# Output products regrouped by kind, and the first two periods of an attention stage rearranged

## The chip, the cores and the metric

The kernel runs on one core of one Trainium2 chip. The metric is device time in microseconds: the median of several executions. A profiled execution has a span (first to last instruction) and a time of its own, which is a little longer.

## The reference

The kernel computes a linear attention with exponential features and, behind it, a two-layer block. The two weight matrices of the block arrive as float64.

```python
# q, k, v: (8 batches, 8 heads, 576 positions, 64); w_phi: (64, 128)
def phi(x):
    proj = einsum('bhsd,df->bhsf', x, w_phi)
    proj = proj - max(abs(proj), axis=-1)
    return concatenate([exp(proj), exp(-proj)], axis=-1)
q_p, k_p = phi(q), phi(k)
kv = einsum('bhsf,bhsd->bhfd', k_p, v)
z = sum(k_p, axis=2)
num = einsum('bhsf,bhfd->bhsd', q_p, kv)
den = einsum('bhsf,bhf->bhs', q_p, z) + 1e-06
x = (num / den), laid out as (4608, 512)
h = x @ w_in            # (512, 2048)
out = (h - tanh(h)) @ w_out
```

## The kernel before

**Two stages.** The attention takes roughly the first third of the time, the two-layer block the rest. Only the attention is touched.

**Units.** A unit is one batch and two heads (index e); there are 32 (`NU`). Its input `qk` holds the transposed queries and keys of both heads, 64 partitions a head and 2 x 576 columns; `v` holds the values. A unit's work goes through three periods of one loop, `for i in range(NU + 2)`: in period i, unit i (`a`) is projected, unit i-1 (`c`) is turned, summed and exponentiated, and unit i-2 (`p`) gets its outputs. The loop runs under a manual schedule: every engine takes its instructions in the order in which the loop writes them, and SP, which issues all transfers, takes them in that order too.

**One period's steps, by engine.**

- `project(a, r)`, r = 0, 1, 2: on TensorE six float32 products, which the profile shows as twelve instructions, into the one PSUM tile `pp`; then on VectorE a maximum of absolute values (`m`) and a subtract (`t`). As there is one tile `pp`, block r+1 on TensorE waits for the subtract of block r.
- `k_exp` (ScalarE): exponents of the keys, into `kp`. Its second half, `k_exp(c, 2)`, is issued in the next period.
- `kv(c)` (TensorE): keys times values, twenty instructions, needs all of `kp`. `ksum(c)`: sums of the keys' features.
- `qt`, `qt_rest`, `q_exp` (TensorE and ScalarE): transposes of the queries and their exponents `qe`, for both signs s and both heads e.
- `kv_copy`, `kv_turn`: ScalarE copies the keys-times-values out of PSUM, TensorE transposes them, VectorE copies the result to `kv`.
- `out_heads(p)` (TensorE): for each sign s, the numerators (L265: two column halves c and two heads e, 64 output columns each, PSUM tiles 0 and 1) and then the denominators (L275: four strips of 32 columns of PSUM tile 2). Each is accumulated over s. A float32 product shows as two instructions, so a block of four is eight.
- `out_copy`, `den`, `den_recip`, `den_mul`: copies to SBUF, a transfer `dn`, a reciprocal, a transfer out (`rr`) and two back (`rb`), a product on GpSimd and the store of x to DRAM (`xs`). The second stage reloads x from there.
- `dec_load`, `dec_0`, `dec_1`, `dec_2`: in each period one block of a float64 weight is loaded (`raw`, two buffers) and turned into float32: one ScalarE operation, then three of VectorE (`dec_1`), then one more of VectorE (`dec_2`). All 32 blocks are done within the attention.

**The start.** `wph` (the two copies of w_phi) is loaded first, then `qk` of unit 0, its `v`, and two weight blocks. Eight products of a tile of zeros, `zt`, are pinned in front of everything on TensorE (L134, bfloat16, 256 columns, into the PSUM tile `pw`, which nobody reads).

Of the kernel before, what the change touches and what calls it, by code (L numbers as in the profile page):

```python
# [32 lines left out]
def tile_linear_attention_moe(  # L33
# [73 lines left out]
    def x_split(xt, c, order=lambda ins: ins):  # L107
        xh, xl, x = xt
        order(nc.scalar.copy(xh[:, c, :], x[c]))
        order(nc.vector.tensor_tensor(xl[:, c, :], x[c], f32(xh[:, c, :]), ALU.subtract))  # L110
# [5 lines left out]
    with ExitStack() as c1:  # L116
# [6 lines left out]
        ps_c = c1.enter_context(tc.tile_pool(name="ps_c", bufs=1, space=PSUM))  # L123
        ps_d = c1.enter_context(tc.tile_pool(name="ps_d", bufs=3, space=PSUM))

        wph = p1.tile([P, F], F32, name="wph")
        nc.sync.dma_start(wph[0:D, :], w_phi)
        nc.sync.dma_start(wph[D:P, :], w_phi)
        zt = p1.tile([P, 256], BF16, name="zt")
        nc.gpsimd.memset(zt, 0.0)  # L130

        pw = ps_d.tile([P, 512], F32, tag="po", name="warm")
        for _ in range(8):
            pin(nc.tensor.matmul(pw[:, 0:256], zt[:, 0:P], zt, start=True, stop=True))  # L134

        ones = p1.tile([P, 32], F32, name="ones")
        nc.vector.memset(ones, 1.0)
# [5 lines left out]
        def dec_load(n):  # L143
            u = Dec()
            u.nm = f"{'io'[n % 2]}{n // 2}"
            u.f, u.d = n // 2, (wi, wo)[n % 2]
            u.r = raw.tile([P, DM], U64, tag="raw", name=f"raw{u.nm}")
            if n % 2 == 0:
                nc.sync.dma_start(
                    u.r.rearrange("p (c f) -> p c f", f=P),  # L150
                    w_in[:, u.f * P : (u.f + 1) * P].rearrange("(c p) f -> p c f", p=P),
                )
            else:
                nc.sync.dma_start(u.r, w_out[u.f * P : (u.f + 1) * P, :])
            return u

        def dec_0(u):
            rr = u.r.bitcast(U32).rearrange("p (n t) -> p n t", t=2)
            u.lo, u.hi = rr[:, :, 0], rr[:, :, 1]
            u.a = raw.tile([P, DM], U32, tag="dec_a", name=f"dec_a{u.nm}", bufs=2)  # L160
            nc.scalar.activation(f32(u.a), f32(u.hi), AF.Abs, scale=65536.0)

        def dec_1(u):
            a = u.a
            nc.vector.tensor_scalar(f32(a), f32(a), CMIN, CMAX, ALU.max, ALU.min)
            nc.vector.tensor_scalar(a, a, 3, None, ALU.logical_shift_left)
            nc.vector.scalar_tensor_tensor(a, u.lo, 29, a, ALU.logical_shift_right, ALU.bitwise_or)

        def dec_2(u):
            w = wpool.tile([P, DM], F32, tag="w", name=f"w{u.nm}")  # L170
            nc.vector.scalar_tensor_tensor(
                w.bitcast(U32), u.hi, 0x80000000, u.a, ALU.bitwise_and, ALU.bitwise_or
            )
            u.d[u.f] = w
# [3 lines left out]

        def load(u):
            u.qk = p2.tile([P, PC], F32, tag="qk", name=f"qk{u.i}")  # L180
            nc.sync.dma_start(u.qk, qkT[u.i])

        def load_v(u):
            u.v = p2.tile([P, 5, 2, D], F32, tag="v", name=f"v{u.i}")
            nc.sync.dma_start(u.v.rearrange("p j e d -> p (j e d)"), v5[u.i])


        def project(u, r):
            pp = ps_pj.tile([P, 2, 512], F32, tag="pj", name=f"pp{u.i}_{r}")
            for a in range(3):  # L190
                j = 3 * r + a
                for e in range(2):
                    hs = slice(e * D, (e + 1) * D)
                    nc.tensor.matmul(  # L194
                        pp[:, e, a * F : (a + 1) * F], u.qk[hs, j * P : (j + 1) * P], wph[hs, :], start=True, stop=True
                    )
            x = pp[:, :, 0 : 3 * F].rearrange("p e (a f) -> p e a f", f=F)
            m = p2.tile([P, 2, 3], F32, tag="m", name=f"m{u.i}_{r}")
            nc.vector.tensor_reduce(m, x, AX.X, ALU.max, apply_absolute_value=True)  # L199
            t = p2.tile([P, 2, 3, F], F32, tag=f"t{r}", name=f"t{u.i}_{r}")  # L200
            nc.vector.tensor_tensor(t, x, m.unsqueeze(3).broadcast_to([P, 2, 3, F]), ALU.subtract)  # L201
            u.t[r] = t
# [28 lines left out]
        def kv(u):  # L231
            u.pc = ps_c.tile([P, 512], F32, tag="pc", name=f"pc{u.i}")
            for j in range(5):
                r = slice(SR, P) if j == 0 else slice(0, P)
                for e in range(2):
                    nc.tensor.matmul(  # L236
                        u.pc[e * D : (e + 1) * D, 0 : 2 * F], u.v[r, j, e, :], u.kp[r, e, j, :, :], start=(j == 0), stop=(j == 4)
                    )
# [21 lines left out]
        def out_heads(u):  # L260
            u.po = [ps_d.tile([P, 512], F32, tag="po", name=f"po{u.i}_{c}") for c in range(3)]
            for s in range(2):
                for c in range(2):
                    for e in range(2):
                        nc.tensor.matmul(  # L265
                            u.po[c][e * D : (e + 1) * D, 0:CH],
                            u.kv[:, s, e * D : (e + 1) * D],
                            u.qe[:, e, s, c * CH : (c + 1) * CH],
                            start=(s == 0),
                            stop=(s == 1),  # L270
                        )
                for e in range(2):
                    for c in range(2):
                        n, w = 2 * e + c, 2 * e + s
                        nc.tensor.matmul(  # L275
                            u.po[2][n * 32 : (n + 1) * 32, 0:CH],
                            u.kv[:, 2, w * 32 : (w + 1) * 32],
                            u.qe[:, e, s, c * CH : (c + 1) * CH],
                            start=(s == 0),
                            stop=(s == 1),  # L280
                        )
# [27 lines left out]
        def den_mul(u, pin=lambda ins: ins):  # L309
            x = u.rb  # L310
            pin(nc.gpsimd.tensor_tensor(x, u.d, x, ALU.mult))  # L311
            nc.sync.dma_start(xs[u.b // 2][u.hp, :, (u.b % 2) * S : (u.b % 2 + 1) * S], x)
# [7 lines left out]
        NU = len(units)  # L320
        assert NU == 2 * NF
        load(units[0])
        load_v(units[0])
        dec = [dec_load(0), dec_load(1)]
        def unit(i):
# [3 lines left out]
        with tc.manual_schedule():  # L329
            for i in range(NU + 2):  # L330
                a, c, p, p2_ = unit(i), unit(i - 1), unit(i - 2), unit(i - 3)
                if i + 1 < NU:
                    load(units[i + 1])
                    load_v(units[i + 1])
                if i == NU:
                    xt = {0: x_tiles(0)}
                    for j in range(NCT):
                        x_load(0, xt[0], j)
                if a:
                    a.kp = p2.tile([P, 2, 5, 2, F], F32, tag="kp", name=f"kp{i}")  # L340
                    project(a, 0)
                if c and i < NU:
                    k_exp(c, 2)
                if p:
                    out_heads(p)
                if c and i == NU:
                    k_exp(c, 2)
                if i < NU:
                    dec_0(dec[i])
                    dec_1(dec[i])  # L350
                if p:
                    out_copy(p)
                    den(p)
                if p2_:
                    den_mul(p2_)
                if a:
                    project(a, 1)
                if c:
                    kv(c)
                if a:  # L360
                    k_exp(a, 1)
                if i < NU:
                    dec_2(dec[i])
                if i + 2 < NU:
                    dec.append(dec_load(i + 2))
                if i == NU:
                    for j in range(NCT):
                        x_split(xt[0], j)
                if a:
                    project(a, 2)  # L370
                if c:
                    c.qe = p1.tile([P, 2, 2, S], F32, tag="qe", name=f"qe{i - 1}")
                    pt = qt(c, 0)
                    q_exp(c, 0, pt)
                    ksum(c)
                    ptr = qt_rest(c)
                    kv_copy(c)
                    q_exp_rest(c, ptr)
                    pt = qt(c, 1)
                    kv_turn(c)  # L380
                    q_exp(c, 1, pt)
                if p:
                    den_recip(p)
                if i == NU:
                    split_w(0)
            for f in range(1, AHEAD):
                split_w(f)
# [150 lines left out]
```

## Time and profile before

| | us |
|---|---|
| median of 3 executions (lowest, highest) | 1226.46 (1226.25, 1227.1) |
| profiled execution, its time | 1227.16 |
| profiled execution, its span | 1225.4 |
| TensorE busy (matmul) | 1192.7 |
| VectorE busy | 895.6 |
| ScalarE busy | 800.9 |
| GpSimd busy | 273.2 |

In the profile PE is TensorE's products, PEld its weight loads, DVE VectorE, ACT ScalarE, POOL GpSimd, SP the engine that issues transfers. Starts are microseconds from the span's start, and L265 is line 265 of the kernel. Products are pipelined, so that the durations of neighbours overlap and the step from start to start is the better price. The chain of waits follows the last instruction back, at each step to what released it.

### The profile page before, as it was taken

The numbers are of one execution on the slowest core, as the hardware profiler recorded it, in microseconds if no ns is written. First come the engines' busy times: TensorE is split into PE (matmuls) and PEld (weight loads), VectorE is DVE, ScalarE is ACT, GpSimd is POOL, SyncE is SP. The second block draws the span as 40 slices with busy tenths as digits, with TensorE's granted clock in tenths as the row PEclk, the third lists the DMA queues.
The fourth block names the chain that finished last, engine by engine and source line by source line (L and its number), as shares of the span: only waits on it lengthen the run. The fifth ranks groups of instructions, "written<-read, shape, count | busy, mean of one in ns | idle before, by whom it ended". The sixth has DMA issues, their size and how long they took to land.

```text
span 1225.4 us, 22381 instructions
## 1 busy us (share of the span) xinstructions
PE 1192.7 (97%) x8552; PEld 962.8 (79%) x8552; DVE 895.6 (73%) x1478; ACT 800.9 (65%) x1709; POOL 273.2 (22%) x253
## 2 busy tenths in 40 slices
PE   5999999999999799999999999999999999999998
PEld 4565665665655688999999999999999999999997
DVE  5778778877775898767777777677677777777765
ACT  2665665656655676767776776776676776776665
POOL 0011111110111653222222222222222222222222
PEclk9999999999999999999999999999999999999999
DMA  4465566655653100001010000000010100000000
GB/s 157 123 195 169 172 186 177 175 174 166 199 164 113 45 14 29 20 11 39 14 40 14 33 20 33 14 33 20 7 39 14 39 14 33 21 26 1 27 1 27
DMA packets 50892, 85.70 MB, mean 70 GB/s; under 512 B 13280, under 2 KB 27744, under 8 KB 50784
## 3 DMA queue, kind: packets, MB, share of 16 engines
q1 hardware_dynamic: 50784, 84.27, 22.4%
q8 instruction: 67, 1.10, 0.4%
q14 instruction: 41, 0.34, 0.1%
HBM read 65.08 MB, written 19.02 MB: 69 GB/s over the span
## 4 chain that ended last, share of the span: by engine, by line
PE 92%; DVE 4%; ACT 1%; DMA 1%; issue 1%; SPq 0%; DVEq 0%
PE ph L407 31%; PE po L441 10%; PE po L442 10%; PE po L444 10%; PE pp L194 7%; PE pc L236 6%; PE po L265 5%; PE pc L244 3%; PE po L275 3%; PE ptt L207 3%; DVE s L424 1%; PE ptk L255 1%; PE ptr L213 1%; DVE s L428 1%; DVE s L423 0%
## 5 line engine op out<-in xcount | busy, mean ns | idle before, releaser
L435 POOL TENSOR_TENSOR gl<-s,gh 128x384 fp32r<-128x384 f32 x192 | 197.2, 1027 | 592.9 <-ACT gh L434 582.2
L407 PE MATMUL ph<-xh,wli 128*128 128x384 f32 x768 | 259.7, 338 | 3.5 <-POOL wli L92 3.5
L407 PE MATMUL ph<-xh,whi 128*128 128x384 f32 x768 | 259.3, 338 | 0.9 <-DVE th L427 0.9
L407 PE MATMUL ph<-xl,whi 128*128 128x384 f32 x768 | 258.5, 337 | 0.0
L414 ACT ACTIVATE y<-ph 128x384 f32<-128x384 f32 x192 | 94.3, 491 | 231.9 <-PE ph L407 231.9
L441 PE MATMUL po<-who,gh 128*128 128x512 f32 x576 | 228.7, 397 | 7.9 <-ACT gh L434 7.8
L423 DVE SCALAR_TENSOR_TENSOR s<-s,y 128x384 f32<-128x384 f32 x192 | 111.0, 578 | 166.9 <-ACT s L416 166.8
L442 PE MATMUL po<-wlo,gh 128*128 128x512 f32 x576 | 227.5, 395 | 0.0
L444 PE MATMUL po<-who,gl 128*128 128x512 f32 x576 | 164.1, 393 | 0.0
L407 PEld LDWEIGHTS ph<-xh,whi 128*128 128x128 f32 x768 | 144.8, 188 | 10.1 <-issue 1.7
L428 DVE COPY_PREDICATED s<-mk,th 128x384 f32<-128x384 uint32 x192 | 136.5, 711 | 20.0 <-DVE th L427 0.5
L407 PEld LDWEIGHTS ph<-xl,whi 128*128 128x128 f32 x768 | 144.6, 188 | 8.2
L407 PEld LDWEIGHTS ph<-xh,wli 128*128 128x128 f32 x768 | 144.5, 188 | 4.3 <-POOL wli L92 4.2
L228 ACT ACTIVATE kp<-t 128x768 f32<-128x768 f32 (+1 forms) x128 | 87.2, 733 | 68.5 <-DVE t L201 68.5
L199 DVE TENSOR_REDUCE m<-pp 128x6 f32<-128x768 f32 x96 | 91.8, 956 | 54.0 <-PE pp L194 53.9
L441 PEld LDWEIGHTS po<-who,gh 128*128 128x128 f32 x576 | 108.2, 188 | 28.8 <-ACT gh L434 11.7
L422 ACT ACTIVATE mk<-y,bias_t 128x384 f32<-128x384 f32 x192 | 117.8, 613 | 19.0 <-DVE s L428 19.0
L424 DVE SCALAR_TENSOR_TENSOR s<-s,s 128x384 f32<-128x384 f32 x192 | 115.1, 599 | 18.9 <-ACT mk L422 0.9
L444 PEld LDWEIGHTS po<-who,gl 128*128 128x128 f32 x576 | 108.4, 188 | 25.3
L311 POOL TENSOR_TENSOR rb<-d,rb 128x576 f32<-128x576 f32 x32 | 47.2, 1474 | 347.8 <-DMA rb<-rr 344.1
L442 PEld LDWEIGHTS po<-wlo,gh 128*128 128x128 f32 x576 | 108.6, 189 | 16.5
L416 ACT ACTIVATE s<-y,bias_t 128x384 f32<-128x384 f32 x192 | 118.4, 617 | 0.0
(63 smaller groups left out, 1660.8 us busy)
## 6 DMA issues: line engine op xcount, KB each, us to landing
qk<-in_qkT SPq DMA_DIRECT2D x32, 576.0 KB, 4.8
v<-in_v SPq DMA_DIRECT2D x32, 320.0 KB, 8.0
rb<-rr SPq DMA_DIRECT2D x64, 144.0 KB, 2.9
xs<-rb SPq DMA_DIRECT2D x32, 288.0 KB, 2.1
x<-xs SPq DMA_DIRECT2D x48, 192.0 KB, 2.3
out<-o SPq DMA_DIRECT2D x36, 256.0 KB, 2.1
rawi<-in_moe_w_in SPq DMA_DIRECT2D x16, 512.0 KB, 4.4
rawo<-in_moe_w_out SPq DMA_DIRECT2D x16, 512.0 KB, 4.5
```

The source lines that it names most:

```text
L199: nc.vector.tensor_reduce(m, x, AX.X, ALU.max, apply_absolute_value=True)
L407: nc.tensor.matmul(h, wt[:, c * P : (c + 1) * P], x[:, c, 0:N], start=(i == 0), stop=(i == 3 * NCT - 1))
L414: nc.scalar.activation(y, h, AF.Square)
L416: nc.scalar.activation(s1, y, AF.Square, bias=bias_t[:, 0:1])
L422: nc.scalar.activation(mk, y, AF.Relu, bias=bias_t[:, 2:3])
L423: nc.vector.scalar_tensor_tensor(s1, s1, PC1, y, ALU.add, ALU.mult)
L424: nc.vector.scalar_tensor_tensor(s2, s2, PC2, s1, ALU.add, ALU.mult)
L428: nc.vector.copy_predicated(gs, mk.bitcast(U32), th)
L435: pin(nc.gpsimd.tensor_tensor(gl, gs, f32(gh), ALU.subtract))
L441: nc.tensor.matmul(po[t], a, wo[f][0], start=(f == 0), stop=False)
L442: nc.tensor.matmul(po[t], a, wo[f][1], start=False, stop=False)
L444: nc.tensor.matmul(po[t], gl[:, t * P : (t + 1) * P], wo[f][0], start=False, stop=(f == NF - 1))
```

## The change

Four things are changed. In `out_heads` the numerators of both signs are issued first, then the denominators of both. The load of unit 0's `qk` goes in three transfers, ahead of `wph`. The products of zeros are no longer pinned at the start: 16 stand in front of the first projection, 8 behind it, 8 before unit 0's third block, and 8 behind unit 1's first block. And in periods 0 and 1 the decode of the weights stands behind the third block of the projection, and `kv(0)` ahead of unit 1's second block; the third and fourth weight blocks' loads move with the decode.

```diff
--- before.py
+++ after.py
@@ -123,15 +123,15 @@
         ps_c = c1.enter_context(tc.tile_pool(name="ps_c", bufs=1, space=PSUM))
         ps_d = c1.enter_context(tc.tile_pool(name="ps_d", bufs=3, space=PSUM))
 
-        wph = p1.tile([P, F], F32, name="wph")
-        nc.sync.dma_start(wph[0:D, :], w_phi)
-        nc.sync.dma_start(wph[D:P, :], w_phi)
         zt = p1.tile([P, 256], BF16, name="zt")
         nc.gpsimd.memset(zt, 0.0)
 
+
         pw = ps_d.tile([P, 512], F32, tag="po", name="warm")
-        for _ in range(8):
-            pin(nc.tensor.matmul(pw[:, 0:256], zt[:, 0:P], zt, start=True, stop=True))
+
+        def warm(n):
+            for _ in range(n):
+                nc.tensor.matmul(pw[:, 0:256], zt[:, 0:P], zt, start=True, stop=True)
 
         ones = p1.tile([P, 32], F32, name="ones")
         nc.vector.memset(ones, 1.0)
@@ -178,7 +178,9 @@
 
         def load(u):
             u.qk = p2.tile([P, PC], F32, tag="qk", name=f"qk{u.i}")
-            nc.sync.dma_start(u.qk, qkT[u.i])
+            w = PC if u.i else 3 * P
+            for o in range(0, PC, w):
+                nc.sync.dma_start(u.qk[:, o : o + w], qkT[u.i][:, o : o + w])
 
         def load_v(u):
             u.v = p2.tile([P, 5, 2, D], F32, tag="v", name=f"v{u.i}")
@@ -269,6 +271,7 @@
                             start=(s == 0),
                             stop=(s == 1),
                         )
+            for s in range(2):
                 for e in range(2):
                     for c in range(2):
                         n, w = 2 * e + c, 2 * e + s
@@ -320,6 +323,9 @@
         NU = len(units)
         assert NU == 2 * NF
         load(units[0])
+        wph = p1.tile([P, F], F32, name="wph")
+        nc.sync.dma_start(wph[0:D, :], w_phi)
+        nc.sync.dma_start(wph[D:P, :], w_phi)
         load_v(units[0])
         dec = [dec_load(0), dec_load(1)]
         def unit(i):
@@ -338,6 +344,8 @@
                         x_load(0, xt[0], j)
                 if a:
                     a.kp = p2.tile([P, 2, 5, 2, F], F32, tag="kp", name=f"kp{i}")
+                    if i == 0:
+                        warm(16)
                     project(a, 0)
                 if c and i < NU:
                     k_exp(c, 2)
@@ -345,7 +353,7 @@
                     out_heads(p)
                 if c and i == NU:
                     k_exp(c, 2)
-                if i < NU:
+                if 2 <= i < NU:
                     dec_0(dec[i])
                     dec_1(dec[i])
                 if p:
@@ -353,21 +361,32 @@
                     den(p)
                 if p2_:
                     den_mul(p2_)
+                if i < 2:
+                    warm(8)
+                if c and i == 1:
+                    kv(c)
                 if a:
                     project(a, 1)
-                if c:
+                if c and i > 1:
                     kv(c)
                 if a:
                     k_exp(a, 1)
-                if i < NU:
+                if 2 <= i < NU:
                     dec_2(dec[i])
-                if i + 2 < NU:
+                if 2 <= i < NU - 2:
                     dec.append(dec_load(i + 2))
                 if i == NU:
                     for j in range(NCT):
                         x_split(xt[0], j)
+                if i == 0:
+                    warm(8)
                 if a:
                     project(a, 2)
+                if i < 2:
+                    dec_0(dec[i])
+                    dec_1(dec[i])
+                    dec_2(dec[i])
+                    dec.append(dec_load(i + 2))
                 if c:
                     c.qe = p1.tile([P, 2, 2, S], F32, tag="qe", name=f"qe{i - 1}")
                     pt = qt(c, 0)
```

## Rows read from the trace of the kernel before

**Rows 1.** The page's chain that ended last: shares of the span by engine.

```profile
PE 92%; DVE 4%; ACT 1%; DMA 1%; issue 1%; SPq 0%; DVEq 0%
```

**Rows 2.** Waits of PE, 33 to 384 us: total us, times, longest.

```profile
PE po L265 <- DVE kv L257: 0.7, 1, 0.7
```

**Rows 3.** Busy time by stretch, one period: PE, PEld, DVE, ACT, POOL, clock, DMA, GB/s.

```profile
138.00:149.68 11.68, 11.68 (x143) 7.12 (x141) 8.96 (x14) 7.19 (x16) 1.42 (x1) 1.00 0.59 179
```

**Rows 4.** Timeline of PE, narrow stretches in out_heads: start, duration, instruction.

```profile
44.35 0.46 PE L265 MATMUL po<-qe,kv 128*64 128x288 f32 x2
44.65 0.41 PE L265 MATMUL po<-qe,kv 128*64 128x288 f32 x2
...
45.13 0.41 PE L265 MATMUL po<-qe,kv 128*64 128x288 f32 x2
45.48 0.45 PE L275 MATMUL po<-qe,kv 128*32 128x288 f32 x4
45.74 0.43 PE L275 MATMUL po<-qe,kv 128*32 128x288 f32 x4
46.10 0.46 PE L265 MATMUL po<-qe,kv 128*64 128x288 f32 x2
```

**Rows 5.** Timeline, 16 to 50 us: the last query exponents, a projection block.

```profile
43.27 1.08 ACT L218 ACTIVATE qe<-ptt 128x512 f32<-128x512 f32 x2
43.49 0.94 PE L194 MATMUL pp<-wph,qk 64*128 64x128 f32 x12
```

**Rows 6.** The chain in order of time, 0 to 70 us: start, duration, what.

```profile
2.00 4.00 DMA qk<-in_qkT
...
6.13 1.67 PE pp L194 x12
...
7.82 0.97 DVE m L199
...
9.78 0.14 issue
...
22.88 4.66 PE pc L236 x20
27.54 1.21 PE pp L194 x12
...
31.88 0.87 PE pp L194 x12
32.75 1.12 PE po L265 x8
...
37.10 2.46 PE pc L236 x20
```

**Rows 7.** Timeline, 0 to 50 us: first issue, zeros, decode, exponent, copy.

```profile
0.74 0.57 SPq L127 DMA_DIRECT2D wph<-in_w_phi  x1
1.34 1.89 PE L134 MATMUL warm<-zt 128*128 128x256 bf16 x8 [1.34 <-POOL zt L130]
9.88 0.43 DVE L165 TENSOR_SCALAR dec_ai<-dec_ai 128x512 f32<-128x512 f32 x1
13.47 0.68 DVE L171 SCALAR_TENSOR_TENSOR wi<-rawi,dec_ai 128x512 uint32<-128x512 uint32 x1
17.38 1.58 ACT L228 ACTIVATE kp<-t 128x768 f32<-128x768 f32 x2 [2.64 <-DVE t L201]
31.92 0.56 DVE L257 COPY kv<-ptk 128x384 f32<-128x384 f32 x1 [1.17 <-PE ptk L255]
```

**Rows 8.** The tile wph: time from issue to landing.

```profile
DMA to landing us min/median/max: 2.0/2.1/2.1
```

**Rows 9.** The chain, 384 to 445 us: the reload of x.

```profile
386.98 3.75 DMA x<-xs
```

**Rows 10.** Busy time by stretch, 424 to 432 us; columns as in rows 3.

```profile
424.00:428.00 4.00, 1.56 (x8) 1.01 (x7) 3.97 (x10) 1.31 (x3) 0.22 (x1) 0.95 0.00 0
428.00:432.00 4.00, 4.00 (x13) 3.24 (x14) 3.90 (x8) 3.37 (x9) 2.15 (x2) 0.63 0.01 4
```

## The prediction

> **What bounds the kernel now.** I read the chain of waits on the page first. The reader is to see that TensorE carries 92% of the chain that ended last, so what counts is time on TensorE or a wait of TensorE [rows 1]. Then TensorE's waits inside the attention: between 33 and 384 us it waited once, for 0.7 us [rows 2]. One period of the attention is 11.68 us, and the stretch table shows TensorE busy for all of it, VectorE for 8.96 and ScalarE for 7.19 us [rows 3]. So in those thirty periods every nanosecond taken off TensorE counts until one of the others gets in the way. The first 33 us are different. There the chain alternates: twelve projection products on TensorE (1.67 us), then about 1.96 us of VectorE's reduce and subtract, then the next twelve [rows 6]. And the products are slow: 1.67 us for a block that takes 0.87 us from 32 us on, 4.66 us for the keys-times-values block that takes 2.46 later [rows 6]. The column of the granted clock says 1.00 there, but a factor of nearly two for the same instructions is the clock at the lower of its two levels (1.2 and not 2.4 GHz), until about 28 us.
>
> **The change, part by part.**
>
> *Order of out_heads.* Nothing is added or removed; 16 numerator products (64 output columns each) and 16 denominator products (32 columns) are issued as 16 + 16 instead of 8 + 8 + 8 + 8. The narrow timelines give single steps. Numerators run two at a time: four pairs, the first at 44.35, the second at 44.65, the fourth at 45.13, then the denominators start at 45.48. So a pair follows a pair at 0.24 us (0.48 for the two steps from 44.65 to 45.13), but the first step after a switch is 0.30 and the step into the next kind 0.35. Denominators run four at a time: starts at 45.48 and 45.74, the next kind at 46.10: 0.26 and 0.36 [rows 4]. Before, one unit costs 2 x (1.13 + 0.62) = 3.50 us. After, the numerators are eight pairs: 0.30 + 6 x 0.24 + 0.35 = 2.09; the denominators four quadruples: 0.26 + 2 x 0.25 + 0.36 = 1.12 (0.25 is chosen between the 0.24 of a pair and the 0.26 seen; no run of quadruples is longer than two before). Sum 3.21, saving 0.29 us; with 0.26 it is 0.27, with 0.24 and a 0.30 that was also part of the switch it is 0.31.
>
> What is late next? The second half of the numerators now begins 1.02 us after the first and not 1.75, and wants the second exponent of the queries, which ends at 44.35, as the first half begins [rows 4, 5]: 1.0 us to spare. The next projection starts 0.29 earlier and wants VectorE's subtract, which follows the previous block by 0.94 + 1.96 + 0.14 = 3.04 us [rows 5, 6], against 0.87 + 3.21 = 4.08 on TensorE: over 1 us to spare. ScalarE's copies start at the end of the denominators as before. So the 0.29 us comes through whole.
>
> For how many of the 32 units? The hand-over to the second stage hangs on the reload of x, which is queued on SP behind the denominator transfers of unit 29 and landed at 390.7 us [rows 9]; the two output blocks after that one have idle TensorE time beside them. So 30 units: 30 x 0.29 = **8.8 us** (8.1 to 9.3).
>
> *First load.* SP issues wph, wph, qk; then qk in three, wph, wph. Issues come 0.63 us apart (0.74 to 2.00 for two) [rows 6, 7]. Now wph's second half is fifth: 0.74 + 4 x 0.63 = 3.26, plus 2.1 to landing [rows 8] = 5.36, and the products start at about 5.45 instead of 6.13. The thirds of qk are issued from 0.74 on instead of 2.00, so they are in by then. v and the two weight loads are issued 1.26 us later; v is first wanted at 17 us, the weights at 15. Gain 0.7 us (0 if the three smaller transfers hold up wph, 0.9 at best).
>
> *Products of zeros, and the rearranged periods.* Eight such products took 1.89 us cold [rows 7]; 16 take 3.8 and end at 5.1, before the data. The groups of 8 stand in waits of 2.1 us (9.92 - 7.80): covered, cold or not. What they are worth hangs on when the clock rises. Before, TensorE was busy 44% of each 3.78 us in that stretch and it stayed low; it rose some 7 us into work that had begun at 21.2. After, from 1.34 us on there are only short breaks: 3.8 us of zeros, then 1.67 + 1.89 of each 3.78. I take it that the first block is still cold and the rest warm; bounds below.
>
> Warm, a cycle is 3.78 - (1.67 - 0.94) = 3.05 us. Blocks of unit 0 at 5.45, 9.23, 12.28; unit 1's first at 15.33. VectorE now decodes the first weights only here, behind the third subtract: 2 x 0.43 + 0.69 (estimated as long as the last step) + 0.68, some 2.3 us with gaps [rows 7], until 17.5, while TensorE does block (0.87), eight zeros (about 0.95) and keys-times-values (2.46; the exponent that it waits for, 1.58 us [rows 7], is done at 16.8) until 19.6. Reduce and subtract end at 17.5 + 1.96 = 19.5: the decode is hidden, with 0.1 us to spare. Second block 19.6, a bare wait (the product that filled it has moved ahead), third block at 22.7. Then 0.87, the transposes and sums (28.75 to 31.88 before, 3.13 us), 0.87 for the next block: TensorE is ready for the first outputs at 27.5. But VectorE has subtract until 25.6, then the second decode of 2.3 us, and only then the copy of kv (0.56): 28.5. This is a new wait of 1.0 us, queued behind it the outputs and all that follows on TensorE. First outputs at 28.6 and not 32.75: gain **4.1 us**, the 0.7 of the load in it.
>
> Bounds: all warm from the first block 4.8. If the clock falls once again, in the idle 2.1 us before unit 1's blocks, about 1.7 us less: after 424 us TensorE was busy 1.56 of 4.00 us, fell to a granted clock of 0.63 in the next 4 us, and 3.4 us at half speed cost 1.7 [rows 10]. If it doesn't rise before keys-times-values: unit 1 begins at 16.8, block 1.67, zeros 1.89, product 4.66, second block at 25.0, the outputs at 33.9: 1.2 us lost.
>
> *Sum.* 8.8 + 4.1 = 12.9 us from the profiled 1227.16 (span 1225.4 and 1.76 around it) gives 1214.3. The profiled execution is 0.7 above the median 1226.46, so the timed median should be **1213.6**.
>
> **Rivals.**
> 1. *The clock rises late or falls again.* For it: the eight zeros before did not lift it, and bare waits remain. Against: the breaks get much shorter. Startup gains 1 to 3 us: 1214.5 to 1216.7; with the clock not lifted at all (the products of zeros don't do what they are there for) 1226.46 - 8.8 + 1.2 = 1218.9.
> 2. *The order is worth nothing.* If each product's weight load is exposed, the steps of 0.35 and 0.36 are loads and not switches, and 16 products in one run cost as much as 8 + 8: only the start gains, 1226.46 - 4.1 = 1222.4. Against it: within a run each pair has its own loads and still follows at 0.24. The Trainium skill (TensorE: Matmul & The Clock Gate, Part 3: Packing small matmuls) says that a weight load overlaps matmuls in flight only where the row group differs. All these products use the full 128 rows, so by that rule it is this case; the trace, with 0.24 us a pair, disagrees.
> 3. *Slower.* The second half of the numerators waits for the second exponent, in each of 30 periods. Place: ScalarE's queue, where that exponent stands behind three other operations. It decides from 1.0 us of lateness on; each further 0.1 us costs 3.0. To eat 12.9 us it must be 1.45 us late: at 1.5, 30 x 0.48 - 12.9 = 1.5 us slower, 1228. Against: in the trace it is 0.0 late [rows 4, 5], and ScalarE has 4.5 us idle a period.
> 4. *The hand-over goes otherwise.* If the fall at 424 us [rows 10] doesn't come in the shifted schedule, 1.7 less: 1211.9; one fall more is as much the other way.
>
> **How the numbers follow.** Forecast (1213.6, own range 1212 to 1215) 0.48; rival 1 0.27, of it 0.07 without any lift; rival 2 0.12; rival 3 0.03; rival 4 0.10, half to each side. The range: low end with 9.3 and 4.8 at their best and something of rival 4, 1211.0; high end with rival 1 whole, 1219.0. Left out are rivals 2 and 3 and a little at the low end, under 0.2. A difference of 0.2% (2.5 us) is about what a measurement of this kernel tells from none. All but rival 3 and a rest of rival 2 are faster by more: 0.95; 0.02 the same; 0.03 slower.
>
> **What would show it.** Order: in one period 16 numerator products in 2.09 and 16 denominator products in 1.12 us, and a period of 11.39 instead of 11.68; a wait of TensorE for ScalarE's exponent there would be rival 3, steps over 0.3 us within the runs rival 2. Start: first projection at 5.45, the later blocks at 0.94 and not 1.65 us; keys-times-values of unit 0 in 2.5; a wait of about 1 us for the copy of kv before the first outputs, at 28.6. Blocks of 1.65 after 10 us would be rival 1. The forecast is wrong if the period stays above 11.5 us or the first outputs start after 31 us.

## The result, and the profile after

The changed kernel takes 1214.86 us (median of 5 executions, 1213.98 to 1215.98), against 1226.46 before: ratio 0.9903, 95% interval 0.989 to 0.9917. The profiled execution took 1214.86 with a span of 1213.1 us, 12.3 less than the span before.

The chain of the page, TensorE's waits between 33 and 372 us, and one period of the attention (columns as in [rows 1 to 3]):

```profile
PE 90%; DVE 5%; DMA 2%; issue 1%; ACT 1%; SPq 0%; DVEq 0%
```

```profile
PE po L267 <- DVE kv L259: 0.7, 1, 0.7
PE pp L196 <- DMA qk<-in_qkT: 0.4, 1, 0.4
```

```profile
160.00:171.39 11.39, 11.39 (x145) 7.30 (x143) 8.72 (x14) 7.17 (x15) 1.41 (x1) 1.00 0.61 189
```

The period is 11.39 us and TensorE is still busy for all of it: what the order saved was passed on whole. One wait is new, 0.4 us for the load of queries and keys. The timeline of out_heads in one period, to be read beside [rows 4] (start, duration, instruction):

```profile
40.99 0.46 PE L267 MATMUL po<-qe,kv 128*64 128x288 f32 x2
...
41.28 0.66 PE L267 MATMUL po<-qe,kv 128*64 128x288 f32 x4
...
42.50 0.66 PE L267 MATMUL po<-qe,kv 128*64 128x288 f32 x4
...
43.08 0.45 PE L278 MATMUL po<-qe,kv 128*32 128x288 f32 x4
...
43.84 0.43 PE L278 MATMUL po<-qe,kv 128*32 128x288 f32 x4
...
44.19 0.94 PE L196 MATMUL pp<-wph,qk 64*128 64x128 f32 x12
```

Sixteen numerator products take 43.08 - 40.99 = 2.09 us and sixteen denominator products 44.19 - 43.08 = 1.11. From the second pair of numerators to the seventh it is 42.50 - 41.28 = 1.22 us, 0.24 a step; on the way the PSUM tile changes three times. The fourth quadruple starts 0.76 after the first, 0.25 a step.

The start, by the chain in order of time (columns as in [rows 6]):

```profile
2.12 3.02 DMA wph<-in_w_phi
...
5.26 1.73 PE pp L196 x12
7.00 1.82 PE warm L134 x8
...
9.09 1.65 PE pp L196 x12
10.74 0.98 PE warm L134 x8
...
12.82 0.95 PE pp L196 x12
...
17.77 2.46 PE pc L238 x20
...
23.23 0.94 PE pp L196 x12
24.17 0.92 PE ptt L209 x4
25.09 2.45 PE pc L246 x40
...
29.67 2.09 PE po L267 x16
```

Eight products of zeros take 1.82 us on the chain, the next eight 0.98: the clock rose between the second projection block and the third. But the transposes at 24.17 take 0.92 us where later periods take 0.59, and the sums behind them 2.45 instead of 1.36. The stretch table (columns as in [rows 3]) shows why:

```profile
20.00:24.30 4.30, 2.16 (x29) 1.72 (x27) 2.00 (x3) 1.18 (x3) 0.00 (x0) 1.00 0.81 313
24.30:27.70 3.40, 3.40 (x46) 2.21 (x45) 3.28 (x5) 1.72 (x4) 0.00 (x0) 0.50 0.00 0
```

The granted clock is 0.50 from 24.3 to 27.7 us, the level of 1.2 GHz, after TensorE stood still for 2.1 us ahead of the block at 23.23. An equal wait ahead of the block at 15.85 was not followed by a fall. The first outputs start at 29.67 us instead of 32.75 [rows 6].

Then the hand-over to the second stage, by the chain and in two lines of the stretch table:

```profile
371.87 1.40 DMA rr<-rn
...
375.57 3.53 DMA x<-xs
...
382.79 3.77 PE po L267 x16
...
390.17 0.18 DVE rn L304
...
390.59 1.57 DVE who L90 x2
...
393.83 1.45 DVE s L443
```

```profile
384.00:388.00 4.00, 4.00 (x32) 1.81 (x29) 0.00 (x0) 0.26 (x1) 2.01 (x2) 0.74 0.34 113
416.00:420.00 4.00, 4.00 (x14) 3.46 (x13) 3.90 (x7) 3.36 (x9) 2.01 (x3) 0.60 0.00 0
```

Added up along the kernel: 3.08 us at the first outputs; 11.07 at the outputs of unit 29 (29 periods of 11.39 against 11.68, less 0.50 in the one period with the late load); 11.63 at the end of the reload of x (390.73 against 379.10 [rows 9]); 11.04 at the addition just ahead of the last reciprocal (401.21 against 390.17), because the clock fell again (0.74 on average from 384 to 388 us) and the last unit's numerators took 3.77 us; 12.2 at VectorE's second operation behind the casts `who` (406.03 against 393.83), because these two casts took 1.57 instead of 2.75 us on the chain; and 12.2 to 12.3 from there to the end.

### The profile page after: what moved, and what is told of

Read it like the earlier page. It is cut to its first block, busy times and chain, and to the rows that moved or that the text cites. A ratio compares the mean times of both kernels' runs of the same rounds, so it can differ in the third digit from the quotient of the medians.

```text
span 1213.1 us, 22447 instructions
## 1 busy us (share of the span) xinstructions
PE 1186.4 (98%) x8584; PEld 969.9 (80%) x8584; DVE 890.8 (73%) x1478; ACT 800.6 (66%) x1709; POOL 272.6 (22%) x253
## 4 chain that ended last, share of the span: by engine, by line
PE 90%; DVE 5%; DMA 2%; issue 1%; ACT 1%; SPq 0%; DVEq 0%
PE ph L426 31%; PE po L461 10%; PE po L460 10%; PE po L463 10%; PE pp L196 7%; PE pc L238 6%; PE po L267 5%; PE pc L246 3%; PE ptt L209 3%; PE po L278 3%; DVE s L443 1%; PE ptk L257 1%; DVE s L447 1%; PE ptr L215 1%; DVE s L445 1%
```

## The experiments

Ratios are to the kernel before, run on the same chip in the same series.

**Only the order** (load, zeros and first periods as before):

```diff
                             stop=(s == 1),
                         )
+            for s in range(2):
                 for e in range(2):
                     for c in range(2):
                         n, w = 2 * e + c, 2 * e + s
```

> Only the order of the output products is changed; load, zeros and the first two periods are as before. If each switch between numerators and denominators costs about 0.15 us (steps of 0.30, 0.35 and 0.36 instead of 0.24 to 0.26), the period of the attention is 11.39 us as in the changed kernel, thirty periods give 8.8 us, and the time is 1217.7 us (ratio 0.9928); the first outputs start at 32.7 us as before. Rival: the steps are weight loads that no order hides, and the shorter period of the changed kernel came with its start: period 11.68, time 1226.5, ratio 1.000.

Measured: 1218.1 us, ratio 0.9925 (0.9909 to 0.9942). The chain shows the period, 11.39 us between the outputs of two units:

```profile
65.98 2.09 PE po L265 x16
...
77.37 2.09 PE po L265 x16
```

The order alone does it; the rival is out. The first outputs started at 31.8 and not 32.7 us, since the clock happened to rise 2.5 us earlier (25.7 instead of 28.2).

**Only the start** (the changed kernel with the loop over s joined again).

> The changed kernel with the old order of the output products. If the two parts add up, the period is 11.68 us, the first outputs start at 29.6 us instead of 32.7 (3.1 us), and the time is 1223.4 us (ratio 0.9975), give or take 1.5 for falls of the clock in the hand-over to the second stage. Rival: the start's gain is taken back later (by transfers or by the hand-over): time 1226.5, ratio 1.000.

Measured: 1224.21 us, ratio 0.9976 (0.9964 to 0.9988). Two lines of the chain, and one of the stretch table:

```profile
65.89 1.12 PE po L267 x8
...
77.57 1.12 PE po L267 x8
```

```profile
14.00:18.00 4.00, 2.95 (x19) 2.39 (x20) 3.90 (x6) 1.58 (x2) 0.00 (x0) 0.50 0.01 4
```

The period is 11.68, and the parts add up: 0.9925 x 0.9976 = 0.9901, against 0.9903 for both. But the start went another way than in the changed kernel: the clock rose at 7.2 us, after one slow block, and fell again at 14.0, in the bare wait that follows unit 0's third block (13.0 to 15.0), and stayed low until 20.8. First outputs at 30.8.

**Only the load.**

```diff
+        load(units[0])
         wph = p1.tile([P, F], F32, name="wph")
         nc.sync.dma_start(wph[0:D, :], w_phi)
```

> Before, with the first load in three transfers ahead of the two of w_phi, and nothing else. The first projection starts at 5.3 us instead of 6.1; its block takes 1.67 us as before, and every later block of unit 0 too. If the load's 0.87 us is passed on whole, the first outputs start at 31.9 us, and the load is 0.9 of the 3.1 us of the start. Rival: the clock rises at a moment of its own and takes the gain away or doubles it: first outputs anywhere between 30 and 33.5.

Measured, in one execution: 1226.2 us. The chain:

```profile
5.15 1.79 PE pp L193 x12
...
31.51 1.12 PE po L264 x8
```

Unit 0 starts 0.98 us earlier (6.13 [rows 6]), all its blocks are cold, and the first outputs come 1.24 earlier; 0.3 of that came from the clock (unit 1's last block took 0.93 instead of 1.21). So the load is some 0.9 us of the start, read from the trace alone: the time lies among those of the kernel before in the same series (1225.63 to 1228.3).

**Few zeros** (the three later groups left out, 8 instead of 16 at the start; the rearranged periods stay).

```diff
                     if i == 0:
-                        warm(16)
+                        warm(8)
...
-                if i < 2:
-                    warm(8)
...
-                if i == 0:
-                    warm(8)
```

> The changed kernel with only 8 products of zeros, all ahead of the first projection; the other 32 are left out, the rearranged periods stay. If it is the zeros in the waits that lift the clock, the blocks of unit 0 take 1.65 us up to the last, keys-times-values of unit 0 takes over 4 us, and the first outputs start at 32.0 to 32.6 us, some 2.7 us later than in the changed kernel (time about 1217.5). Rival: the rearrangement and the load alone do it: blocks of 0.94 us by 13 us and first outputs at 29.6 to 30, time 1214.9.

Measured: 1217.88 us, ratio 0.9922 (0.9907 to 0.9937). The chain:

```profile
5.12 1.78 PE pp L196 x12
...
16.46 1.65 PE pp L196 x12
18.12 4.57 PE pc L238 x20
...
32.13 2.08 PE po L267 x15
```

As the theory had it: all blocks cold, keys-times-values cold, the first outputs 2.5 us later than in the changed kernel. Without the zeros the start is worth 0.6 us (32.75 to 32.13), less than the load gives alone (0.9). What the rearrangement is worth by itself is not shown by this: here too the clock fell, at 25.9 us behind a bare wait, and unit 1's last block, the transposes and the sums behind it took 1.52, 1.04 and 1.82 us instead of 0.94, 0.59 and 1.36. The 1.2 us lost that the prediction set as a bound did not come either, mostly since the zeros that stood between unit 1's first block and keys-times-values are gone here (1.89 us cold).

**All waits filled.** The clock had fallen after bare waits; this puts eight products of zeros into the two that were left. Each then has 1.1 of its 2.1 us bare, like the others.

```diff
-                if i == 0:
+                if i < 2:
                     warm(8)
                 if a:
                     project(a, 2)
+                if i == 0:
+                    warm(8)
```

> The changed kernel with 8 more products of zeros in each of the two waits that it left bare: behind unit 0's third block and ahead of unit 1's third block. If it is the bare waits that let the clock fall (24.3 us in the changed kernel, 14.0 us with the old output order), it now stays up from the time it has risen (by 11 us): the transposes and sums before the first outputs take 3.1 us and not 4.6. TensorE is then ready for the first outputs at about 28.1 us, but VectorE still has the second decode in front of the copy of kv, so they start at 29.0 us after a wait of 0.9 us: 0.6 us better than the changed kernel, time 1214.3. Rival: the falls have nothing to do with the waits: a fall again somewhere before 28 us, first outputs at 29.6 or later.

Measured: 1212.76 us, ratio 0.9882 (0.9867 to 0.9897). The clock rose at 4.9 us and did not fall before the first outputs. The timeline of the first outputs:

```profile
26.23 0.69 DVE L171 SCALAR_TENSOR_TENSOR wo<-rawo,dec_ao 128x512 uint32<-128x512 uint32 x1
...
26.84 0.55 DVE L259 COPY kv<-ptk 128x384 f32<-128x384 f32 x1
...
27.44 2.16 PE L267 MATMUL po<-qe,kv 128*64 128x288 f32 x16 [0.76 <-DVE kv L259]
```

Here is the wait that the prediction had put at 1.0 us: 0.76, behind the second decode. The first outputs came 1.6 us earlier than expected, as the clock rose before the first block and not after it.

**Filled, and the decode moved.**

```diff
                 if a:
                     project(a, 1)
+                if i == 1:
+                    dec_0(dec[i])
+                    dec_1(dec[i])
...
                     kv_turn(c)
+                    if i == 1:
+                        dec_2(dec[i])
+                        dec.append(dec_load(i + 2))
```

> As the one with all waits filled, and the second weight block's decode taken apart: its first four operations stand behind unit 1's second subtract, its last one behind the copy of kv. If that decode is what the first outputs wait for once the clock stays up, they now start at 28.1 us, right behind the projection block before them, 1.5 us better than the changed kernel: 1213.4 us. Rival: the next wait is VectorE's reduce of unit 2 behind the moved decode (the 0.9 us come back one block later): first outputs at 28.1, but the second outputs at 40.4 instead of 39.5, and time 1214.3.

Measured: 1211.8 us, ratio 0.9876 (0.9861 to 0.9891). The first outputs start without a wait, and 29 periods of 11.39 us follow:

```profile
26.88 2.16 PE L267 MATMUL po<-qe,kv 128*64 128x288 f32 x16
```

They start 1.2 us before the time that was expected, as the clock rose within the first block, at 6.0 us. The rival is out. All four executions (1211.53 to 1212.78) lie below all four of the changed kernel in the same series (1213.26 to 1216.49). This version beats both kernels.

**One change of kind more** (denominators, numerators of both signs, denominators).

```diff
+            dens(0)
             for s in range(2):
                 nums(s, 0)
                 nums(s, 1)
+            dens(1)
```

> The changed kernel with the output products as denominators, numerators of both signs, denominators: four changes of kind around and in the outputs, where the changed kernel has three and the kernel before five. If each change costs the same 0.147 us (half of 11.68 - 11.39), the period is 11.54 us. Rival: what counts is that the numerators are in one run (all of the gain): 11.39; or that the denominators are (none of it): 11.68.

Measured, in one execution: 1221.09 us. The chain, and the period of 77.40 - 65.88 = 11.52 us:

```profile
65.88 0.62 PE po L278 x8
66.50 2.09 PE po L266 x16
...
77.40 0.62 PE po L278 x8
```

**Three changes of kind more** (for each sign: half of the numerators, denominators, the other half).

```diff
             for s in range(2):
                 nums(s, 0)
+                dens(s)
                 nums(s, 1)
```

> The changed kernel with the output products, for each sign, as half of the numerators, the denominators, the other half of the numerators: six changes of kind around and in the outputs, one more than the kernel before and three more than the changed one. At 0.147 us each the period is 11.39 + 3 x 0.147 = 11.83 us, 0.15 above the kernel before; the time, at thirty periods, about 1228. Rival: the cost is not by the change of kind but by the sign (a second half that waits for its exponent, or for the first half's accumulation): then 11.68 as before.

Measured, in one execution: 1226.94 us; the period is 76.68 - 64.85 = 11.83:

```profile
64.85 0.64 PE po L266 x4
65.49 0.62 PE po L278 x8
...
76.68 0.64 PE po L266 x4
```

Three, four, five and six changes give 11.39, 11.53, 11.68 and 11.83 us: steps of 0.14 to 0.15 us, 0.147 on average. The sign plays no part.

**The changed kernel again.**

> The changed kernel once more, beside the others on the same chip: ratio 0.990. If the moment at which the clock rises is chance, the first outputs start elsewhere than at 29.6 us, by up to 2 us; if it is fixed by the work, they start at 29.6 again.

Measured: 1215.29 us, ratio 0.9899 (0.9882 to 0.9915). The clock rose at 5.6 us and not at 10.6, and fell at 15.8 and not at 24.3:

```profile
15.80:19.20 3.40, 3.40 (x18) 1.53 (x17) 2.61 (x4) 0.18 (x1) 0.00 (x0) 0.50 0.33 92
```

The first outputs started at 29.14 us, 0.5 earlier. TensorE waited twice for the load of queries and keys, 0.9 us together, and once 1.2 us for a reciprocal on VectorE. And the wait for the copy of kv that the prediction had is here:

```profile
29.14 1.19 PE L267 MATMUL po<-qe,kv 128*64 128x288 f32 x8 [0.76 <-DVE kv L259]
```

The executions with only the start and with three changes more have it too, 0.76 us in each. In all three the clock was up from 21 us on.

**Queries and keys a period earlier** (on top of the moved decode).

```diff
-            u.qk = p2.tile([P, PC], F32, tag="qk", name=f"qk{u.i}")
+            u.qk = p2.tile([P, PC], F32, tag="qk", name=f"qk{u.i}", bufs=3)
...
-                if i + 1 < NU:
-                    load(units[i + 1])
+                if i == 0:
+                    load(units[1])
+                if i + 1 < NU:
                     load_v(units[i + 1])
+                if i + 2 < NU:
+                    load(units[i + 2])
```

> The version with all waits filled and the decode moved, and the load of queries and keys issued a whole period earlier, into a third buffer. In the runs with the period of 11.39 us, TensorE waited now and then for that load (0.2 to 0.9 us in an execution), in those with 11.68 never. If that is what the shorter period exposes, no period is now longer than 11.39 and no wait for that load is left; the time falls by 0 to 0.9 us against 1211.8, most in the executions that are above the median. Rival: the third transfer at the start gets in the way of the first weight block or of the values, and the first outputs start later than 26.9 us: 1212.5 or more.

Measured: 1212.0 us, ratio 0.9876 (0.9859 to 0.9892). TensorE's waits from 25 to 370 us:

```profile
PE pp L196 <- DVE t L203: 0.8, 1, 0.8
PE po L267 <- DVE kv L259: 0.6, 1, 0.6
```

The wait for the load is gone, but the version without this step had none either in its profiled execution, and the time is the same. One period was 12.31 us, with 0.8 of it a wait for a subtract on VectorE. So that the third buffer takes the load's waits away is not shown, and if it gives time, that is too little to be measured here. The rival is out: the first outputs started at 26.7 us.

## Why the prediction was right

**Order.** Right, and nearly to the digit: 2.09 and 1.11 us where 2.09 and 1.12 were worked out, 11.39 for the period, 30 periods. The step of 0.25 for denominators was the one seen. 8.8 us were forecast; 8.3 are left in the profiled execution after the one period with a late load. That period is what the prediction missed. It had looked at what VectorE and ScalarE could spare, and not at the load of queries and keys, which stands on SP behind a transfer that must land first: in the late case SP stood 4.1 us for it. In the periods of 11.39 us such waits came to 0.4, 0.2, 0, 0.2, 0 and 0.9 us (changed kernel, order only, few zeros, all filled, decode moved, changed kernel again); no profiled execution with periods of 11.53 us or more shows one.

**First load.** 0.87 us on the path instead of 0.7 (5.26 against 5.45 forecast). Two sizes were off and nearly cancelled: the issues of the small transfers come 0.46 us apart and not 0.63, while w_phi, now issued behind the queries and keys, landed 3.0 us after its issue and not 2.1.

**Zeros.** The mechanism was right: without them the blocks stay cold. The size was off: 3.1 us at the first outputs instead of 4.1. The forecast had one cold block and no fall; the profiled execution had two cold blocks and one fall, 0.7 and 1.5 us (0.92 + 2.45 + 0.35 against 0.59 + 1.36 + 0.26). That is what rival 1 described: the start's 3.1 us and the time, 1214.86, lie at the edge of its ranges (1 to 3 us, 1214.5 to 1216.7) as well as inside the forecast's own. It is the rule rather than the exception: in all six profiled executions in which a bare wait followed the rise (the changed kernel twice, only the start, few zeros, one and three changes more) the clock fell again before 33 us; in none of the three with filled waits did it. Not every such wait was followed by a fall: of eleven bare waits of 2.1 us with the clock up, in those six executions, seven were and four were not.

**The new wait for the copy of kv.** Forecast at 1.0 us, not there in the profiled execution: the fall of the clock had delayed TensorE by more than that. Where the clock was up ahead of the outputs it appears, 0.76 us, in the changed kernel's second profiled execution as well. So in the first one two errors partly covered each other, which is luck: 0.7 and 1.5 us lost to the clock, against 1.0 for a wait that did not come and 0.2 at the load, make the 1.0 us by which the start fell short.

**Hand-over.** Not forecast in detail. Its sum was +0.8 us to the good: a fall of the clock in the last unit's numerators cost 0.6, and two casts of VectorE were 1.2 us shorter. GpSimd was at work during all of the longer casts and during about 1.1 of the 1.57 us of the shorter; that its work is what made them long is argued and wasn't tried. The total came within 0.6 us of the forecast (12.3 against 12.9 in the profiled executions) partly by luck: the start gave 1.0 less, the periods 0.5 less, and the hand-over, which the sum did not have, gave 0.8 back.

**Rivals.** 2 is out by the two kernels with more changes of kind: the weight loads are the same in all four, and the time goes with the changes. The rule of the Trainium skill (TensorE: Matmul & The Clock Gate, Part 3: Packing small matmuls), that loads overlap only products of another row group, does not hold here: sixteen products on the same 128 rows, each with its own load, follow at 0.24 us a pair. 3 is out: no period waits for an exponent. Of 4, the fall that the kernel before had at 424 us came again in the profiled execution (0.60 from 416 to 420 us), and one fall more, between 380 and 388, cost 0.6. The order is the larger part (0.75% of 0.97%), the start the smaller (0.24%).

## What to carry to other kernels

Where products of different kinds alternate, count the changes of kind and multiply by the price of one, read from the steps at a switch; regrouping cost nothing here, as the operand that moves forward was ready. Where products of zeros are to hold the clock, put them into every wait of the stretch: a single bare wait of 2.1 us lost the clock in seven of eleven cases, for 3.4 to 6.8 us. And when a period gets shorter, look at the transfer queue too: which load stands behind a transfer that must land, and how much it has to spare.

## What the runs showed of the hardware

- A change of kind between numerators (64 output columns) and denominators (32) costs 0.147 us on average. The change of PSUM tile is not what costs: within the numerators it comes at 0.24 us a pair too. Whether it is the number of columns was not separated from what else differs, and the price of a change to or from the projection was not measured alone.
- Pairs of numerator products follow at 0.24 us with a weight load each, in runs of 16 as in runs of 8.
- The moment at which the clock rises is not fixed by the work: with the same 16 zeros from 1.34 us on it rose at 4.2, 4.5, 4.9, 5.6, 5.7, 6.0, 7.2 and 10.6 us (estimates from the durations of the products in eight executions; 5.6 and 10.6 are the same kernel).
- The column of the granted clock can say 1.00 where products take nearly twice their time: it did so until 28 us in the kernel before. The durations tell.
